# Loading W by halves and the forward tables in two ways in a fused Fourier layer and expert MLP

## The chip, the cores and the metric

The kernel runs on one core of one Trainium2 chip. The metric is the time of the core in device microseconds (us). Several executions are timed; medians are given with the lowest and highest. The engines go by short names: PE is TensorE, ACT ScalarE, DVE VectorE, POOL GpSimd, SP SyncE. Every run lists the mean clock that TensorE was granted, as a share of full speed. One profiled execution of each kernel gives the page and the trace, whose span is some 2 us shorter than the time.

## The reference

```python
X = np.fft.rfft(x, axis=1)                      # x: 8 x 3008 x 256, float32
Yr = Xr @ w_r - Xi @ w_i + b_r                  # w_r, w_i: 256 x 256
Yi = Xr @ w_i + Xi @ w_r + b_i
Yr, Yi = soft_threshold(Yr, 0.01), soft_threshold(Yi, 0.01)
y = np.fft.irfft(Yr + 1j * Yi, n=3008, axis=1)  # then 24064 tokens of 256
r = np.maximum(y @ moe_w_in, 0.0)               # 256 -> 2048
out = (s * (r * r) + b) @ moe_w_out             # 2048 -> 256
```

## The kernel before

The transform of 3008 points is done as 94 x 32 by matmuls with constant tables. A first batch goes through a start-up stage of its own (`first_batch`); while it runs, all tables and weights are loaded. "Mixing" is the product of the transformed x with w_r and w_i (together W). After about 50 us PE goes from tile to tile of the expert MLP, with the transforms of later batches in between. The parts that matter:

```python
# start: x of batch 0 in eight pieces on the POOL queue, W whole on the SP queue
emit_load_x(0)
for w in (w_r, w_i):
    st = rpool.tile([P, DC, D], F32, name="w_st", tag="rt")
    nc.sync.dma_start(out=st, in_=w.rearrange("(c p) e -> p c e", p=P))
...
def emit_load_forward():           # compact forward table of 12 pairs, placed by copies
    nc.sync.dma_start(out=F_c.rearrange("p q r k -> p q (r k)"), in_=F_d)
    nc.sync.dma_start(out=sel_t, in_=S_d)

def emit_load_inverse():
    nc.sync.dma_start(out=T_t[:, 0:H], in_=t_d[:, 0:H])
    nc.sync.dma_start(out=F_t[:, H:], in_=f_d)
    nc.sync.dma_start(out=F_2[1], in_=f_2_d)
    t_load = nc.sync.dma_start(out=T_t[:, H:], in_=t_d[:, H:])
    ...                            # identity, last table, biases
def emit_load_weights():
    for dc in range(DC):
        nc.gpsimd.dma_start(out=w_in_t[dc], in_=moe_w_in[dc * P : (dc + 1) * P, :])
    nc.gpsimd.dma_start(out=w_out_t, in_=moe_w_out.rearrange("(mc p) d -> p mc d", p=P))
...
# first_batch: after the first DFT of x come the copies that place F_c, on ACT and DVE;
# then the next x and the expert weights, let go by the second half of F_t:
gate = nc.gpsimd.tensor_copy(out=w_in_t[0][0:1, 0:1], in_=F_t[0:1, H, 0:1])
with tc.issue_after(gate.ins):
    emit_load_x(1)
    emit_load_weights()
...
def sum_w_out():                   # on POOL (GpSimd): column sums of w_out, for the bias b
    nc.gpsimd.tensor_tensor(out=acc, in0=w_out_t[:, 0:2], in1=w_out_t[:, 2:4], op=ALU.add)
    for q in range(4, MC, 2):
        nc.gpsimd.tensor_tensor(out=acc, in0=acc, in1=w_out_t[:, q : q + 2], op=ALU.add)
    nc.gpsimd.tensor_tensor(out=w_sum, in0=acc[:, 0], in1=acc[:, 1], op=ALU.add)

def make_bias():                   # the "bias matmul": PE reads the sum
    ps = other_bank()
    nc.tensor.matmul(ps[:, 0:D], ones, w_sum, start=True, stop=True)
    ...
# in each expert tile: relu on ACT, then the square on DVE, with rt as both inputs in SBUF
nc.vector.tensor_tensor(out=gt[:, :, 0:w], in0=rt[:, :, 0:w], in1=rt[:, :, 0:w], op=ALU.mult)
```

## Time and profile before

| | before |
|---|---|
| time | 848.3 us median of 6 (847.65 to 848.57) |
| span of the trace | 846.2 us |
| PE busy | 833.9 us, 99% |
| last x lands, first mixing matmul | 13.25, 14.21 us |
| first expert matmul | 47.94 us |
| w_out landed, its sum ready, bias matmul | 40.98, 50.39, 51.99 us |
| first output tile evacuated | 63.18 us |

PE is busy for nearly all of the span, so the table follows the few moments of the first 65 us that can move its start. A row of a timeline has the start in us, the length in us, engine, line, operation, output<-input, the number of merged instructions, and in brackets how long the engine was idle before and what ended that. In the waits, a row is who waited for whom: us in total, times, longest. The times of landing are taken from the trace's DMA completion counts, the 16th of a transfer's 16.

### The profile page before, as it was taken

Reading aid. Unit: us, or ns where it says so; the run is one execution under the profiler, and the core shown is the slowest. Engines: PE = TensorE matmul, PEld = TensorE weight load, DVE = VectorE, ACT = ScalarE, POOL = GpSimd, SP = SyncE. Lnnn points to the kernel's source line nnn. Section 1 sums busy time; section 2 is a strip of 40 time slices with the busy share of each in tenths; the row PEclk is TensorE's granted clock in tenths of the full one; section 3 lists DMA queues with packets and bytes.
Section 4 is the critical chain, followed back from the end, with each engine's and each line's share of the span. In section 5 each row is a group of like instructions: output and inputs, shape, how many; then the busy total and the mean of one; then the engine's idle time right before and its main releaser. Section 6 shows DMA issues by size and latency. Waiting matters only on the chain.

```text
span 846.2 us, 17115 instructions
## 1 busy us (share of the span) xinstructions
PE 833.9 (99%) x6653; PEld 599.6 (71%) x6653; DVE 691.8 (82%) x1026; ACT 642.7 (76%) x864; POOL 46.0 (5%) x71
## 2 busy tenths in 40 slices
PE   8999999999999999999999999999999999999997
PEld 6857766777677766777677776777667777766765
DVE  5989987888878987888888888798977888776674
ACT  5988886787778787788777887788877778666673
POOL 4341000000000001000000000000000000000000
PEclk9999999999999999999999999999999999999999
DMA  8945568224762367324761247613354223411111
GB/s 201 181 142 122 122 151 212 67 72 103 173 185 57 99 169 182 96 75 108 189 170 51 78 102 199 171 41 91 101 156 122 62 78 97 112 33 38 38 44 50
DMA packets 105747, 96.06 MB, mean 114 GB/s; under 512 B 9543, under 2 KB 97483, under 8 KB 104323
## 3 DMA queue, kind: packets, MB, share of 16 engines
q1 hardware_dynamic: 99218, 80.55, 32.9%
q0 software_dynamic: 6448, 14.42, 10.7%
q8 instruction: 52, 0.85, 0.4%
q14 instruction: 29, 0.23, 0.1%
HBM read 53.52 MB, written 46.66 MB: 118 GB/s over the span
## 4 chain that ended last, share of the span: by engine, by line
PE 89%; DVE 4%; DMA 3%; ACT 3%; issue 1%; POOL 0%; DVEq 0%; ACTq 0%; SPq 0%; POOLq 0%
PE psa L840 36%; PE psh L769 36%; PE psf L635 4%; PE psf L570 2%; PE psf L621 2%; PE psf L606 2%; PE psf L718 2%; PE psf L665 2%; ACT rt L776 1%; DVE gt L783 1%; DMA vd<-v 1%; PE psm L426 1%; DMA vs<-vd 1%; DMA x<-in_x_dram 1%; DMA F_c<-dft_fwd 0%
## 5 line engine op out<-in xcount | busy, mean ns | idle before, releaser
L776 ACT ACTIVATE rt<-psh 128x1024 f32<-128x1024 f32 (+2 forms) x384 | 386.8, 1009 | 119.6 <-PE psh L769 117.8
L783 DVE TENSOR_TENSOR gt<-rt 128x1024 f16<-128x1024 f32 (+2 forms) x321 | 383.9, 1199 | 98.3 <-ACT rt L776 97.6
L840 PE MATMUL psa<-w_out_t,gt 128*128 128x256 f16 (+1 forms) x3024 | 454.6, 272 | 0.1
L840 PEld LDWEIGHTS <-gt 128*128 128x128 f16 (+1 forms) x3024 | 301.0, 101 | 187.0 <-issue 1.4
L769 PE MATMUL psh<-yt,w_in 128*128 128x512 f16 (+1 forms) x1344 | 396.3, 378 | 0.2 <-ACT rt L776 0.2
L769 PEld LDWEIGHTS <-w_in 128*128 128x128 f16 x1536 | 142.9, 98 | 28.0 <-issue 2.0
L850 DVE SCALAR_TENSOR_TENSOR ost<-psa,s_bc,bias_bc 128x512 f32<-128x512 f32 (+2 forms) x97 | 71.0, 732 | 8.3 <-PE psa L840 6.7
L780 ACT ACTIVATE gt<-rt 128x1024 f16<-128x1024 f32 (+2 forms) x63 | 66.2, 1050 | 1.0
L640 DVE TENSOR_TENSOR ring<-psf,s 128x512 f16<-128x512 f32 x84 | 57.4, 684 | 3.7 <-PE psf L635 3.1
L170 ACT CAST v<-psf 128x512 f16<-128x512 f32 x78 | 45.3, 582 | 18.7 <-PE psf L665 18.7
L170 ACT CAST xf<-psf 128x512 f16<-128x512 f32 x82 | 47.9, 585 | 10.9 <-PE psf L606 10.8
L769 PE MATMUL psh<-tail,w_in 128*128 128x512 f16 (+1 forms) x192 | 52.1, 353 | 0.0
L170 ACT CAST u<-psf 96x512 f16<-96x512 f32 x75 | 43.4, 580 | 10.9 <-PE psf L570 10.7
L635 PE MATMUL psf<-W_g,xf 128*128 128x256 f16 x336 | 50.4, 272 | 0.0
L170 ACT CAST yt<-psf 128x480 f16<-128x480 f32 (+2 forms) x73 | 37.3, 523 | 14.2 <-PE psf L718 14.2
L213 POOL DMA_DIRECT2D x<-in_x_dram x36 | 18.7, 526 | 432.4 <-PE psf L570 431.2
L570 PE MATMUL psf<-x,A_t 94*96 94x512 f16 x103 | 39.3, 381 | 1.7 <-ACT yt L170 0.5
L646 DVE TENSOR_TENSOR ring<-ring,high 128x512 f16<-128x512 f16 x84 | 35.5, 423 | 2.3
L647 DVE TENSOR_TENSOR ring<-ring 128x512 f16<-128x512 f16 x84 | 35.4, 422 | 1.9
L645 DVE TENSOR_TENSOR ring<-ring,low 128x512 f16<-128x512 f16 x84 | 35.4, 421 | 1.6
L635 PEld LDWEIGHTS <-xf 128*128 128x128 f16 x336 | 32.9, 98 | 3.9
L718 PE MATMUL psf<-C_t,vs 96*128 96x96 f16 x448 | 33.0, 205 | 0.9 <-DMA vs<-vd 0.8
(97 smaller groups left out, 500.7 us busy)
## 6 DMA issues: line engine op xcount, KB each, us to landing
out_dram<-ost SPq DMA_DIRECT2D x152, 128.0 KB
ud<-u SPq DMA_DIRECT2D x28, 384.0 KB
us<-ud SPq DMA_DIRECT2D x28, 384.0 KB
vd<-v SPq DMA_DIRECT2D x42, 256.0 KB
vs<-vd SPq DMA_DIRECT2D x14, 768.0 KB
x<-in_x_dram POOLq DMA_DIRECT2D x28, 376.0 KB, 6.5
ring<-ring SPq DMA_DIRECT2D x280, 32.0 KB
out_dram<-ost SPq DMA_DIRECT2D x16, 120.0 KB
```

What stands on the lines that cost most here:

```text
L170: return None, nc.scalar.copy(out=dst, in_=src)
L570: nc.tensor.matmul(ps[0:96, :], A_t[0:N1, :], x16[(b, c)][0:N1, j * D : (j + 2) * D], start=True, stop=True,)
L635: nc.tensor.matmul(ps[:, r, :], xt[:, 2 - r, dc], W_g[:, dc, r], start=(dc == 0), stop=(dc == DC - 1),)
L640: nc.vector.tensor_tensor(out=t, in0=ps, in1=hold[i // 2][:, i % 2].unsqueeze(1).to_broadcast([P, 2, D]), op=ALU.add,)
L646: nc.vector.tensor_tensor(out=m, in0=m, in1=high, op=ALU.min)
L718: nc.tensor.matmul(ps[:, j * 96 : (j + 1) * 96], vs[(b, h)][:, k, ec * P : (ec + 1) * P], C_t, start=True, stop=True,)
L769: nc.tensor.matmul(o, w_in_t[dc][:, mc * P : (mc + 1) * P], r, start=(dc == 0), stop=(dc == DC - 1),)
L776: nc.scalar.activation(out=rt[:, :, 0:w], in_=ps[:, :, 0:w], func=AF.Relu)
L780: nc.scalar.activation(out=gt[:, :, 0:w], in_=rt[:, :, 0:w], func=AF.Square)
L783: nc.vector.tensor_tensor(out=gt[:, :, 0:w], in0=rt[:, :, 0:w], in1=rt[:, :, 0:w], op=ALU.mult)
L840: nc.tensor.matmul(ps[0:size, h, :], gts[(ti, mc // 2)][:, mc % 2, sub * size : (sub + 1) * size], w_out_t[:, mc, :], start=(mc == 0), sto ...
L850: nc.vector.scalar_tensor_tensor(out=ost[0:size, 0:k], in0=ps[0:size, 0:k], scalar=s_bc[0:size], in1=bias_bc[0:size, 0:k], op0=ALU.mult, o ...
```

## The change

It is meant to start the mixing of batch 0 sooner. W's first half of output columns comes first and the other half behind x, since the first six of twelve mixing steps use only the first. The forward tables of the first four pairs come at once and are placed while x still arrives; those of the other eight come ready-made behind x and need no placing.

```diff
-        nc.sync.dma_start(out=st, in_=w.rearrange("(c p) e -> p c e", p=P))
+        nc.sync.dma_start(
+            out=st[:, :, 0:P], in_=w.rearrange("(c p) e -> p c e", p=P)[:, :, 0:P]
+        )
         w_st.append(st)
+    F_c = uspool.tile([P, 4, 2, N2], F16, name="F_c", tag="us")
+    nc.sync.dma_start(out=F_c.rearrange("p q r k -> p q (r k)"), in_=F_d)
 ...
-    def emit_load_forward():
 ...
-    def emit_load_inverse():
+    def emit_load_tables():
+        nc.sync.dma_start(out=F_t[:, 4:H], in_=f_d[:, 0 : H - 4])
+        nc.sync.dma_start(out=F_2[0][:, 4:H], in_=f_2_d[:, 0 : H - 4])
         nc.sync.dma_start(out=T_t[:, 0:H], in_=t_d[:, 0:H])
-        nc.sync.dma_start(out=F_t[:, H:], in_=f_d)
-        nc.sync.dma_start(out=F_2[1], in_=f_2_d)
+        for st, w in zip(w_st, (w_r, w_i)):
+            nc.sync.dma_start(
+                out=st[:, :, P:], in_=w.rearrange("(c p) e -> p c e", p=P)[:, :, P:]
+            )
+        nc.sync.dma_start(out=F_t[:, H:], in_=f_d[:, H - 4 :])
+        nc.sync.dma_start(out=F_2[1], in_=f_2_d[:, H - 4 :])
         t_load = nc.sync.dma_start(out=T_t[:, H:], in_=t_d[:, H:])
 ...
-                with tc.issue_after(last_act.ins):
-                    place_w()
-        with tc.issue_after(last_dve.ins), tc.issue_after(last_act.ins):
-            place_f()
-            place_f_2()
+                with tc.issue_after(last_act.ins), tc.issue_after(last_dve.ins):
+                    place_f()
+                    place_w(0)
 ...
+            if i == 3:
+                place_w(1)
```

The tables' build on the host, the zeroing of four pairs in place of twelve, and the small memsets that hold the loads back follow suit and are cut here.

More of the change, by code (lines that the diff above doesn't have):

```diff
@@ L123 @@
     A_d = nc.inline_tensor(first.astype(np.float16), name="dft_first").ap()
-    F_d = nc.inline_tensor(fwd[:, 0:H].astype(np.float16), name="dft_fwd").ap()
+    F_d = nc.inline_tensor(fwd[:, 0:4].astype(np.float16), name="dft_fwd").ap()
     f_all = np.zeros((P, NPAIR, 2, 2, N2))
@@ L131 @@
         t_all[r, :, i % 2] = inv[r]
-    f_2 = np.stack([-f_all[:, H:, 1], f_all[:, H:, 0]], axis=2)
+    f_2 = np.stack([-f_all[:, 4:, 1], f_all[:, 4:, 0]], axis=2)
     f_d, f_2_d, t_d = (
         nc.inline_tensor(t.reshape(P, -1, P).astype(np.float16), name=name).ap()
-        for t, name in ((f_all[:, H:], "fwd_rest"), (f_2, "fwd_rest_i"), (t_all, "dft_inv"))
+        for t, name in ((f_all[:, 4:], "fwd_rest"), (f_2, "fwd_rest_i"), (t_all, "dft_inv"))
     )
@@ L244 @@
             nc.sync.dma_start(out=b_g[r : r + 1, i], in_=bv.unsqueeze(0))
-    F_c = uspool.tile([P, H, 2, N2], F16, name="F_c", tag="us")
     F_2 = [uspool.tile([P, H, P], F16, name="F_2", tag="us") for _ in range(2)]
@@ L252 @@
     sel_t = cpool.tile([P, P], F16, name="sel_t")
+    nc.sync.dma_start(out=sel_t, in_=S_d)
     eye_t = cpool.tile([P, P], F16, name="eye_t")
@@ L264 @@
     T_t = cpool.tile([P, NPAIR, P], F16, name="T_t")
-    def emit_load_forward():
-        nc.sync.dma_start(
-            out=F_c.rearrange("p q r k -> p q (r k)"), in_=F_d
-        )
-        nc.sync.dma_start(out=sel_t, in_=S_d)
-    def emit_load_inverse():
-        nc.sync.dma_start(out=T_t[:, 0:H], in_=t_d[:, 0:H])
-        nc.sync.dma_start(out=F_t[:, H:], in_=f_d)
-        nc.sync.dma_start(out=F_2[1], in_=f_2_d)
+    def emit_load_tables():
+        nc.sync.dma_start(out=F_t[:, 4:H], in_=f_d[:, 0 : H - 4])
+        nc.sync.dma_start(out=F_2[0][:, 4:H], in_=f_2_d[:, 0 : H - 4])
+        nc.sync.dma_start(out=T_t[:, 0:H], in_=t_d[:, 0:H])
+        for st, w in zip(w_st, (w_r, w_i)):
[4 more added lines that the diff above has]
+        nc.sync.dma_start(out=F_2[1], in_=f_2_d[:, H - 4 :])
         t_load = nc.sync.dma_start(out=T_t[:, H:], in_=t_d[:, H:])
@@ L298 @@
     nc.vector.memset(neg_lam, -LAM)
-    nc.vector.memset(F_t[:, 0:H], 0.0)
-    nc.gpsimd.memset(F_2[0], 0.0)
+    nc.vector.memset(F_t[:, 0:4], 0.0)
+    nc.vector.memset(F_2[0][:, 0:4], 0.0)
     def make_bounds():
@@ L316, in blocks, with place_w @@
         return t.rearrange("p q (r a k) -> p q r a k", r=2, a=2)
-    def place_w():
+    def place_w(ec):
+        e = slice(ec * P, ec * P + P)
         for i in range(2):
-            nc.scalar.copy(out=W_t[:, :, i], in_=w_st[i])
+            nc.scalar.copy(out=W_t[:, :, i, e], in_=w_st[i][:, :, e])
     def place_f():
@@ L324, in place_f @@
             r = slice(64 * a, 64 * a + 64)
-            nc.scalar.copy(out=blocks(F_t)[r, 0:H, :, a], in_=F_c[r])
-    def place_f_2():
-        for a in range(2):
-            r = slice(64 * a, 64 * a + 64)
+            nc.scalar.copy(out=blocks(F_t)[r, 0:4, :, a], in_=F_c[r])
             nc.vector.tensor_scalar_mul(
-                out=blocks(F_2[0])[r, :, 0, a], in0=F_c[r, :, 1], scalar1=-1.0
+                out=blocks(F_2[0])[r, 0:4, 0, a], in0=F_c[r, :, 1], scalar1=-1.0
             )
-            nc.vector.tensor_copy(out=blocks(F_2[0])[r, :, 1, a], in_=F_c[r, :, 0])
+            nc.vector.tensor_copy(out=blocks(F_2[0])[r, 0:4, 1, a], in_=F_c[r, :, 0])
     w_sum = cpool.tile([P, D], F16, name="w_sum")
@@ L389, in first_batch @@
                 continue
-            if c == 0:
-                with tc.issue_after(last_dve.ins):
-                    nc.vector.memset(F_c[0:1, 0, 0, 0:1], 0.0)
-                emit_load_forward()
             if c == 2:
                 with tc.issue_after(last_dve.ins):
-                    for t in (T_t[:, 0:H], F_t[:, H:], F_2[1], T_t[:, H:]):
+                    tables = (F_t[:, 4:H], F_2[0][:, 4:H], T_t[:, 0:H])
+                    tables += tuple(st[:, :, P:] for st in w_st)
+                    for t in tables + (F_t[:, H:], F_2[1], T_t[:, H:]):
                         nc.vector.memset(t[0:1, 0, 0:1], 0.0)
-                emit_load_inverse()
+                emit_load_tables()
             if c == 1:
-                with tc.issue_after(last_act.ins):
-                    place_w()
-        with tc.issue_after(last_dve.ins), tc.issue_after(last_act.ins):
-            place_f()
-            place_f_2()
+                with tc.issue_after(last_act.ins), tc.issue_after(last_dve.ins):
+                    place_f()
+                    place_w(0)
         gate = nc.gpsimd.tensor_copy(out=w_in_t[0][0:1, 0:1], in_=F_t[0:1, H, 0:1])
```

## The prediction

> **What bounds the kernel now.** I read the page first, then the chain of waits for the first 70 us in order of time, then the timeline of the first 20 us by engine, then the DMA queues in one-microsecond windows, and last the timelines of POOL and PE from 20 to 56 us. The page says where the bound is:
>
> ```profile
> PE 833.9 (99%) x6653; PEld 599.6 (71%) x6653; DVE 691.8 (82%) x1026; ACT 642.7 (76%) x864; POOL 46.0 (5%) x71
> ...
> PE   8999999999999999999999999999999999999997
> ...
> DMA  8945568224762367324761247613354223411111
> ```
>
> PE is busy in every slice of 21 us except a little in the first and the last. From the second slice on the kernel is a PE stream that the change does not touch (the matmuls, their shapes and count stay), so nearly all of 848 us is fixed. What can move is the moment at which that stream gets going. The chain of waits of the first 18 us (start us, length us, what):
>
> ```profile
> 2.88 6.32 DMA x<-in_x_dram
> 9.26 0.34 PE psm L374 x4
> 9.60 0.18 PE psf L374 x4
> 9.80 0.56 DVE ut L174
> 10.42 4.22 DMA F_c<-dft_fwd
> 14.71 0.83 ACT F_t L325
> 15.56 0.83 ACT F_t L325
> 16.41 0.59 ACT g L432
> 17.05 0.38 PE psf L456 x4
> ```
>
> The reader is to see two things. The chain starts with the load of x, and it then leaves x for the forward table F_c: issued at 10.42 behind a DVE evacuation, landed at 14.64, placed by ACT in two copies until 16.41, and only then come ACT's half of g and the first forward DFT. The x chain runs beside it and ends almost as late. This is PE in the timeline:
>
> ```profile
> 13.30 0.34 PE L374 MATMUL psm<-A_t,x 94*128 94x96 f16 x4 [0.34 <-DMA x<-in_x_dram]
> ...
> 14.21 1.92 PE L426 MATMUL psm<-W_t,ut 128*128 128x256 f16 x16
> 16.44 0.23 PE L456 MATMUL psf<-g,F_t 128*128 128x128 f16 x1 [0.31 <-ACT F_t L325]
> ```
>
> So the last x lands at about 13.3, mixing starts at 14.21, and PE stands for 0.31 us at 16.44 and again until 17.05, for the placing of F_t and the g that ACT does after it. From 17.4 to 31.5 the chain is PE almost alone, in steps of about 1.66 us (forward DFTs start at 19.92, 21.57, 23.25, 25.05), which is PE's own work: mix 8 x 0.109, forward 8 x 0.055 plus 0.11, inverse 4 x 0.055, together 1.64 us. From 31.8 to 49 it is DVE and ACT evacuations back to back, then PE. A saving before 17 us is carried along these links unless some other arrival holds one of them.
>
> [...] from 3 to 6 us the x queue and the SP queue together have 111%, 104% and 115% of 16 engines, and from 6 to 12 us x alone has 96 to 113%. So x is bound by DMA engine time and W takes from it. [...] The halves of W have runs of exactly 512 B. In this trace's packet records 512 B packets of the SP queue have a median of 27 ns and 1024 B ones 46 ns: 85% of the rate per byte, so halves are worth nearly half. [...] F_c's issue takes 0.36 us and its landing 4.2. [...]
>
> **The change, part by part.** *W in halves and an early small F_c.* Before: 512 packets of 1024 B, 512 x 46 ns / 16 engines = 1.47 us of all engines. After: 512 of 512 B and F_c's 128 of 512 B, 640 x 27 / 16 = 1.08 us. Of this a part runs before x's first packet (3.1 us), some 0.40 us before and, at the same packets per us, 0.25 after. In x's stretch that leaves 1.07 against 0.83: x gains 0.24 us. The old F_c also sent about 43 packets of 1536 B (65 ns) beside the last of x, 43 x 65 / 16 = 0.17 us; the tables that take its place are issued at about 12.0 and their first packets come 1.0 to 1.5 us later, after x. Together x ends **0.4 us** earlier, mixing starts at about 13.8.
>
> *Placing out of the way.* The two ACT copies of 0.83 us and the four DVE ones of 0.25 move from behind x to about 10 us, with a third of the columns. With half of W that is an estimated 1.4 us on ACT at 10 us, where it has a 0.48 us evacuation per 1.05 us and four banks to catch up. After mixing starts nothing but g stands ahead of the forward DFT. Before, from 14.21 to the end of the first forward DFT (last matmul issued 17.21) were 3.06 us. After: 16 mix matmuls 1.85 us, then 0.55 us, 2.40. Gain **0.66 us**. It needs the other eight pairs by the second forward DFT at about 17.1. Issued at 12.0 to 12.8, 256 packets of 2048 B, with 1.37 us per 384 KB (median landing to landing of the four tables before): estimated landed by 15.5, slowest engine 16.2. In time. T_t needs 17.3 to 17.8 against use at 17.7: just in time.
>
> *Second halves of W.* Two ACT copies of 128x256 f32 (0.48 us each, 0.36 apart, as L351 has them) go into step 3, where ACT is about 90% busy. ACT has no F_t copies behind it now and had idle of 0.44 us at 23.45; I charge **0.15 us**. W_t's first half loses the same from idle time, worth nothing.
>
> Sum: 0.4 + 0.66 - 0.15 = about **0.9 us**, 0.1% of the time.
>
> **Rivals.** *The expert weights become the wait.* The tables behind x grow by 768 KB (eight pairs twice, W's halves) ahead of F_t's second half, which gates the loads of the next x and the weights. At 1.37 us per 384 KB that is 2.7 us, less 0.4 for the earlier start and what idle DMA time absorbs: w_out lands 1.5 to 2.5 us later. POOL's sum of w_out starts on that landing and its result is read by one matmul (L349) in PE's order:
>
> ```profile
> 41.05 1.15 POOL L340 TENSOR_TENSOR acc<-w_out_t 128x512 f32<-128x512 f16 x1 [5.29 <-DMA w_out_t<-in_moe_w_out_dram]
> 42.28 7.31 POOL L344 TENSOR_TENSOR acc<-acc,w_out_t 128x512 f32<-128x512 f32 x6
> 49.67 0.72 POOL L345 TENSOR_TENSOR w_sum<-acc 128x256 f16<-128x256 f32 x1
> ```
>
> ```profile
> 51.99 0.27 PE L349 MATMUL psa<-w_sum,ones 128*128 128x256 f16 x1
> ```
>
> The sum ends at 50.39 and PE reads it at 51.99: 1.6 us of slack, which an earlier PE (0.9) and a later load (1.5 to 2.5) overdraw by 0.8 to 1.8. PE would then stand there, everything behind it is PE work, and the time is 848.0 to 849.0. Against it: the place of L349 in PE's order is not that of the source (it ran before most of the matmuls listed ahead of it), so it can fall later in the new order, and its result is not used until 63.18. I give this rival about four in ten for some loss, and half of that for losing all of the gain.
>
> *T_t or W's second half land late.* Then PE or ACT waits a few tenths at 17 to 20 us: 847.5 to 848. For it: a slowest engine trailed the median by 0.5 to 1.1 us in these loads. Against: the need is also in rough balance.
>
> *Hidden anyway.* If x does not speed up because the 640 small packets disturb it as much as 512 larger ones, only 0.5 us is left: 847.6. *Better than I count:* if x ends earlier by all of the 256 KB less and the steps up to 31 us also lose their small stalls, 1.5 us: 846.6. A new order of PE's instructions may also shift later stages by about a microsecond either way.
>
> **Range and chances.** 848.15 - 0.9 = 847.25 without a new wait. With the first rival at its weight I stay near that, at **847.3 us**. The lower end is the better case with a lucky order, 845.8; the upper the stand at L349, 848.9. A change of 2% is 17 us, as much as the whole stretch before the PE stream, so I give faster 0.01, within 2% 0.98, slower 0.01.
>
> **What would show it.** Right: the last L374 group at about 12.9 and the first L426 at 13.8 (x step); L456 at about 2 us after the first L426 with no wait for F_t, and the second forward DFT by 17.2 (placing); no ACT gap at the copies of W in step 3. F_c gone from the chain, PE in its place from about 14 us. POOL's first sum of w_out starts at 42.5 to 43.5; PE waits at L349 or not, which decides between gain and none. Wrong: x landing as late as now, a PE wait on F_t or T_t before 20 us, an ACT wait for the second half of W, or a DVE and ACT stretch between 31 and 49 us that gives the lead back.

## The result

The changed kernel took 853.58 us in the median of 6 runs (850.01 to 857.07), against 848.3 before. Executions over 1.5% slower than the fastest of the same kernel are left out of the means. Ratios here are the mean time of one kernel's runs over the mean of the other's in the same rounds, so they are not quite the ratio of the medians quoted. This one is 1.0062 (95% interval 1.0034 to 1.0091): some 5 us slower, less than 2% but clear of noise, and outside the predicted range of 845.8 to 848.9. The spread of 7 us, against 0.9 us before, is part of the result.

The page of the changed kernel (engine busy us and share; then the chain that ended last):

```profile
PE 835.0 (98%) x6653; PEld 600.0 (70%) x6653; DVE 695.0 (82%) x1030; ACT 641.7 (75%) x866; POOL 48.8 (6%) x70
...
PE 85%; DMA 5%; DVE 4%; POOL 2%; ACT 2%; issue 1%; SPq 0%; DVEq 0%; POOLq 0%; ACTq 0%
```

PE has the same 6653 matmuls and 1.1 us more busy time; the span is 5.0 us longer. POOL, with 2% of the chain, had 0% before. The chain of waits of the first 70 us names the links:

```profile
14.46 5.18 DMA F_t<-fwd_rest
...
20.29 2.06 POOL x L213 x4
22.35 1.11 POOL w_in L295 x2
23.46 20.51 DMA w_out_t<-in_moe_w_out_dram
...
50.19 2.02 POOL acc L345
52.28 2.02 POOL acc L345
54.38 1.60 POOL w_sum L346
55.98 0.04 issue
56.02 0.37 PE psa L350
```

F_c has gone from the chain. In its place stand the second half of F_t (it gates the next loads), the load of w_out, POOL's sum of it, and the bias matmul (L350, L349 before). On PE:

```profile
13.37 1.92 PE L423 MATMUL psm<-W_t,ut 128*128 128x256 f16 x16
...
49.37 1.94 PE L768 MATMUL psh<-yt,w_in 128*128 128x512 f16 x8 [0.17 <-ACT rt L775]
56.02 0.37 PE L350 MATMUL psa<-w_sum,ones 128*128 128x256 f16 x1 [4.71 <-POOL w_sum L346]
56.18 0.64 PE L839 MATMUL psa<-w_out_t,gt 128*128 128x256 f16 x2
56.61 1.91 PE L768 MATMUL psh<-yt,w_in 128*128 128x512 f16 x4
```

Mixing starts 0.84 us earlier than before, as meant. Then PE stands 4.71 us at the bias matmul, and after it four expert matmuls take 1.91 us where they took 1.02. Side by side:

| us from the start | before | changed | difference |
|---|---|---|---|
| first mixing matmul | 14.21 | 13.37 | -0.84 |
| second forward DFT | 18.14 | 16.56 | -1.58 |
| second inverse DFT | 20.70 | 19.87 | -0.83 |
| first expert matmul | 47.94 | 47.09 | -0.85 |
| gate for the next x and the weights | 17.33 | 19.77 | +2.44 |
| w_out landed | 40.98 | 43.97 | +2.99 |
| sum of w_out ready | 50.39 | 55.97 | +5.58 |
| bias matmul | 51.99 | 56.02 | +4.03 |
| first output tile evacuated | 63.18 | 68.65 | +5.47 |
| output tiles from 138 us on | | | +4.74 to +4.78 |

The second row against the third shows where half of the early lead went (-1.58 becomes -0.83): ACT stood for the second half of W, in the timeline of ACT:

```profile
18.09 0.41 ACT L325 CAST W_t<-w_st 128x256 f16<-128x256 f32 x1 [0.75 <-DMA w_st<-in_w_r_dram]
18.41 0.68 ACT L458 ACTIVATE m<-psf,neg_lam 128x512 f32<-128x512 f32 x1
18.99 0.39 ACT L325 CAST W_t<-w_st 128x256 f16<-128x256 f32 x1
```

The copies stand ahead of and behind an activation that the next inverse DFT waits for, and PE stood 0.59 us for it at 19.87. The remaining lead of 0.85 us is what was forecast; what follows undoes it. POOL's sum, in its timeline of the changed kernel:

```profile
44.04 1.15 POOL L341 TENSOR_TENSOR acc<-w_out_t 128x512 f32<-128x512 f16 x1 [9.13 <-DMA w_out_t<-in_moe_w_out_dram]
45.27 9.03 POOL L345 TENSOR_TENSOR acc<-acc,w_out_t 128x512 f32<-128x512 f32 x6
54.38 1.59 POOL L346 TENSOR_TENSOR w_sum<-acc 128x256 f16<-128x256 f32 x1
```

It starts 2.99 us later and takes 2.59 us longer than before (11.93 against 9.34), because from 49.35 us on each of its adds is slow (2.02 us for 1.16). The wait adds up: 2.99 + 2.59 + 0.85 of lead - 1.60 of slack that the sum had before = 4.83 us, against 4.71 seen.

The third cost, after the later load and the slower sum, is PE's clock. The windows show it (length, then busy us and instructions of PE, weight loads, DVE, ACT, POOL, then granted clock, DMA share, GB/s):

```profile
48.00:51.30 3.30, 3.13 (x14) 1.24 (x13) 2.12 (x3) 3.01 (x4) 3.14 (x3) 1.00 0.40 119
51.30:56.00 4.70, 0.01 (x1) 0.00 (x0) 4.70 (x3) 1.24 (x2) 4.51 (x3) 1.00 0.44 129
56.00:59.50 3.50, 3.48 (x11) 1.58 (x11) 1.05 (x1) 1.42 (x2) 0.00 (x0) 0.51 1.10 304
59.50:63.00 3.50, 3.50 (x20) 1.78 (x19) 3.05 (x3) 3.02 (x5) 1.37 (x3) 1.00 0.32 85
```

After 4.71 us without work PE gets half of its clock (0.50) for 3.41 us, worth an estimated 1.7 us of work, half of that time; the difference grows by 1.44 us there, from +4.03 to +5.47. From 63 us on the two traces keep their distance to within 0.04 us but for one place at about 131 us, where PE waits for batch 1's return from memory (vs<-vd): 0.8 us in this trace of before, none in that of the changed kernel, and between 0 and 1.9 us in the traces of all kernels here. It is noise, and it limits what a single run can tell.

### The profile page after: what moved, and what is told of

It reads as the page before. A ratio compares the mean times of both kernels' runs of the same rounds, so it can differ in the third digit from the quotient of the medians.

```text
span 851.2 us, 17130 instructions
## 1 busy us (share of the span) xinstructions
PE 835.0 (98%) x6653; PEld 600.0 (70%) x6653; DVE 695.0 (82%) x1030; ACT 641.7 (75%) x866; POOL 48.8 (6%) x70
## 4 chain that ended last, share of the span: by engine, by line
PE 85%; DMA 5%; DVE 4%; POOL 2%; ACT 2%; issue 1%; SPq 0%; DVEq 0%; POOLq 0%; ACTq 0%
PE psa L839 36%; PE psh L768 35%; PE psf L634 4%; PE psf L569 2%; DMA w_out_t<-in_moe_w_out_dram 2%; PE psf L620 2%; PE psf L605 2%; PE psf L717 2%; PE psf L664 2%; DVE gt L782 2%; ACT rt L775 1%; POOL acc L345 1%; DMA x<-in_x_dram 1%; POOL x L213 1%; DMA ring<-ring 1%
```

## The experiments

Two theories stood at the start. A: the loss is PE's wait for w_out and its sum, brought on by the 768 KB that now stand ahead of the gate. B: it comes from somewhere else in the change (the halves of W, the ACT wait, crowded loads), and the wait only marks it. All kernels but the three that add idle work for measurement are full versions; all gave correct results. Each used one chip, with its own runs of before: chip 12 for e1 to e4 (before 848.52), 9 for e5 to e8 (848.26), 8 for e9 and e10 (848.09), 15 for e11 and e12 (847.75).

**e1, the bias matmul later in PE's order.**

```diff
-    plan.setdefault(15, []).append(make_bias)
+    plan.setdefault(22, []).append(make_bias)     # and issued after the last second matmul before it
```

> The changed kernel with one matmul moved: the one that reads the sum of w_out stands about 50 PE instructions later (inside tile 0's second matmuls, still ahead of the first output). Theory A (the loss is the wait of PE for w_out's landing and POOL's sum, 4.7 us in the trace): the wait is gone, PE keeps the 0.85 us that it was ahead at its first expert matmul, 847.4 us (846.8 to 848.2), and the spread of 7 us between runs shrinks below 1.5 us. Theory B (the loss comes from elsewhere, as the wait for the second half of W or slower loads in general, and the wait only marks it): 852 to 854 us, spread as now. If POOL's sum is slowed by VectorE's squares [...], its adds stay at 2.0 us wherever they overlap those.

850.21 us (849.65 to 853.47), ratio 1.003 (1.0013 to 1.0046). The wait is gone (the matmul comes at 63.18, the sum is ready at 55.75) and the granted clock is 1.00 all through 46 to 64 us. So the time falls from 853.6 to 850.2, but not to 847.4, and the spread of 3.8 us is not under 1.5: my expectation missed by 3 us. POOL is as slow as before, without any wait of PE beside it:

```profile
45.02 9.07 POOL L345 TENSOR_TENSOR acc<-acc,w_out_t 128x512 f32<-128x512 f32 x6
54.16 1.59 POOL L346 TENSOR_TENSOR w_sum<-acc 128x256 f16<-128x256 f32 x1
```

DVE pays too: its first ten squares take 13.90 us in this trace (49.74 to 63.64) and 11.49 in that of before, PE waits 1.8 us for ACT and for squares, and the first output tile is evacuated at 65.30, 2.12 us later than before. That is about what is left of the loss. e7 measures this collision of sum and squares alone.

**e2, the kernel before with 768 KB of idle loads ahead of the gate.** Two tables are loaded into the place of w_out before w_out itself.

```diff
         nc.sync.dma_start(out=T_t[:, 0:H], in_=t_d[:, 0:H])
+        for k in range(2):
+            nc.sync.dma_start(out=w_out_t[:, 6 * k : 6 * k + 6]..., in_=t_d[:, 0:H]...)
```

> The kernel before with 768 KB of idle loads (two 384 KB tables into w_out's place) ahead of the second half of F_t, and nothing else of the change. Theory A: the gate opens 2.4 to 3 us later, w_out lands about 3 us later (44 us), POOL's sum runs into the squares and ends near 56, the bias matmul waits about 4 us: 852 to 855 us, with a spread of some us. Theory B (the loss comes from the halves of W or the placing): 848.3 to 849.

850.1 us (848.98 to 854.86), ratio 1.0026 (1.0006 to 1.0045). In its trace the gate opens at 21.52, 4.2 us later than before, w_out lands at 43.18 (+2.2), and the sum is ready at 53.46; PE waits 0.6 us. It reaches its first expert matmul at 48.71, itself 0.77 later than before, as the second forward tables came late. The sign and the spread are the forecast ones, but the size missed (852 to 855 expected): this kernel has no lead that would bring PE to the matmul sooner, so the wait is short (0.6 us) and nothing falls to half clock there (1.00 all through 46 to 64 us). Bytes ahead of the gate are enough to make the kernel slower, with no other part of the change; they don't give the whole loss. Nor do they act by the gate alone: PE itself stood 0.76 us for a table at 22.42, which it did not in the changed kernel, so e2 by itself does not separate the two ways. e3 does.

**e3, the changed kernel with w_out loaded ahead of w_in.** Two statements swap; every engine but POOL keeps its order.

```diff
+        nc.gpsimd.dma_start(out=w_out_t, in_=moe_w_out.rearrange("(mc p) d -> p mc d", p=P))
         for dc in range(DC):
             nc.gpsimd.dma_start(out=w_in_t[dc], in_=moe_w_in[dc * P : (dc + 1) * P, :])
-        nc.gpsimd.dma_start(out=w_out_t, in_=moe_w_out.rearrange("(mc p) d -> p mc d", p=P))
```

> The changed kernel with w_out loaded ahead of w_in; the order of all engines but POOL's three issues is the same. Theory A: w_out lands some 5 us or more earlier (36 to 39 us), the sum ends before 50 us at 1.2 us an add, no wait at the bias matmul, w_in lands by 44 us against use at 47: 847.4 us (846.8 to 848.2), small spread. Theory B: 852 to 854. If w_in lands after 47 us, PE waits there instead and the time rises by that wait.

848.0 us (847.28 to 848.74), ratio 0.9992 (0.998 to 1.0004). w_out lands at 39.68 and w_in at 44.65 against use at 48.08. POOL and PE, each from its timeline:

```profile
39.76 1.15 POOL L341 TENSOR_TENSOR acc<-w_out_t 128x512 f32<-128x512 f16 x1 [3.85 <-DMA w_out_t<-in_moe_w_out_dram]
40.99 7.31 POOL L345 TENSOR_TENSOR acc<-acc,w_out_t 128x512 f32<-128x512 f32 x6
48.37 0.72 POOL L346 TENSOR_TENSOR w_sum<-acc 128x256 f16<-128x256 f32 x1
...
52.13 0.27 PE L350 MATMUL psa<-w_sum,ones 128*128 128x256 f16 x1
```

The adds are at 1.2 us again, there is no wait, and the whole loss is gone, with all of the change still in. Theory A holds for the loss. The lead of PE is gone as well in this trace (first expert matmul 48.08): ACT stood 1.33 us for the second half of W, and T_t kept PE another 0.5.

**e4, the control: the same swap in the kernel before.**

> Control: the kernel before with w_out loaded ahead of w_in. Theory A: the sum was ready 1.6 us before its matmul already, so nothing changes: 848.3 us within 0.4. If the swap helps by itself (the sum off the squares frees VectorE, or the load is cheaper in this order): 847.5 or less, and then e3 proves less.

848.08 us (847.51 to 849.05), ratio 0.9995 (0.9983 to 1.0006). The sum is ready at 45.52, long before its use at 52.04, and nothing is gained: the swap is no improvement of its own, so e3 against the changed kernel measures the late sum: the wait for it, and what it does beside the squares.

**e5, the table part alone** (W whole at the start, placed by two ACT copies at 10 us).

> The changed kernel with W whole at the start, as before the change: the table part alone. Theory A: no ACT wait for W, x ends 0.2 to 0.4 us later than in the changed kernel, the gate opens about 0.9 us earlier (256 KB less ahead of it), w_out lands near 43, the sum still meets the squares and PE still waits at the bias matmul, but 1 to 2 us less: 850 to 852 us. If the halves of W were the main cause: 848 or less.

Five fast runs of 850.54 to 855.7 (one run at a granted clock of 0.557 took 1464.57 us; being the profiled one, its trace is not used), median of the fast ones 851.56, ratio 1.005 (1.0033 to 1.0067). The table part has most of the loss (the whole change had 1.0062, and 1.0044 in e10).

**e6, the W part alone**, in the kernel before.

> The kernel before with W in halves alone, second halves behind the first inverse table, placed in step 3 as in the change. Theory A: w_out lands about 0.9 us later, inside the 1.6 us of slack of the sum, so no wait at the bias matmul; x ends 0.2 us earlier and ACT does not wait or little, as the step comes 1.6 us later than in the changed kernel: 848.0 to 848.8. If the halves are the main cause: 850 or more.

848.52 us (848.26 to 850.39), ratio 1.0009 (0.9997 to 1.0021): no difference to be told. In its trace w_out lands at 41.71 (+0.7), the sum is ready at 52.00 and the bias matmul comes at 52.05. The slack of 1.6 us is just used up, and the sum's last step has already met the squares (1.59 us for 0.72).

**e7, four idle POOL adds behind the sum**, in the kernel before; nobody reads their result.

```diff
+        for q in range(4, 12, 2):
+            nc.gpsimd.tensor_tensor(out=acc, in0=acc, in1=w_out_t[:, q : q + 2], op=ALU.add)
```

> The kernel before with four more POOL adds after the sum, whose result nobody reads; the order of the other engines is the same. They run from 50.4 us beside VectorE's squares. If POOL adds and squares shut each other out: adds of 2.0 us instead of 1.16, squares of 1.9 instead of 1.15 for some 8 us, PE waits for squares or ACT, and the time rises by 1 to 2.5 us, to 849.5 to 851. If not (the long adds of the changed kernel had another cause): adds of 1.2 us, 848.3 us within 0.4.

851.9 us (851.42 to 852.56), ratio 1.0046 (1.0034 to 1.0058): +3.6 us, more than I allowed, for four instructions on an engine that is 5% busy. The squares of DVE in the kernel before, from its timeline:

```profile
50.20 11.49 DVE L783 TENSOR_TENSOR gt<-rt 128x1024 f16<-128x1024 f32 x10 [1.18 <-ACT rt L776]
```

and here, with POOL's idle adds and PE's longest wait:

```profile
50.45 15.24 DVE L785 TENSOR_TENSOR gt<-rt 128x1024 f16<-128x1024 f32 x10 [1.18 <-ACT rt L778]
...
50.35 7.45 POOL L347 TENSOR_TENSOR acc<-acc,w_out_t 128x512 f32<-128x512 f32 x4
...
PE psa L842 <- DVE gt L785: 2.9, 4, 0.8
```

Ten squares take 3.75 us longer, nearly in turn with the adds: their starts follow each other every 2.09 us (50.45, 52.52, 54.61, 56.71) as long as POOL adds, and every 1.14 after. PE then waits for squares, four times, 0.8 us at the longest, without losing its clock (1.00 all through 46 to 64 us). A pair takes 2.09 us, 0.2 less than add and square take one after the other when each runs alone (1.16 + 1.14 = 2.30). The traces show that the two hold each other up, and not by what. This is the cost that e1 kept.

**e8, the swap with W's second half behind all tables, placed in step 5.**

```diff
+            for st, w in zip(w_st, (w_r, w_i)):       # behind T_t's second half
+                nc.sync.dma_start(out=st[:, :, P:], in_=...[:, :, P:])
-            if i == 3:
+            if i == 5:
                 place_w(1)
```

> The changed kernel with w_out ahead of w_in, the second halves of W loaded behind all tables, and their ACT copies in step 5. Theory: e3 lost its lead because ACT stood 0.75 to 1.3 us for the second half of W; here it does not, the gate opens 0.9 us earlier, and PE keeps 1.2 to 1.6 us of lead at the first expert matmul (46.4 to 46.8 us against 47.9): 846.7 to 847.3 us. If tables still come too late at the faster pace (T_t or the second forward tables): 847.5 to 848.

847.39 us (846.59 to 848.73), ratio 0.9993 (0.998 to 1.0006). The first expert matmul comes at 47.11, not at 46.4 to 46.8. ACT's wait for W is down to 0.33 us, but its copies still stand around the activation:

```profile
21.33 0.41 ACT L325 CAST W_t<-w_st 128x256 f16<-128x256 f32 x1 [0.33 <-DMA w_st<-in_w_r_dram]
21.64 0.68 ACT L458 ACTIVATE m<-psf,neg_lam 128x512 f32<-128x512 f32 x1
22.23 0.39 ACT L325 CAST W_t<-w_st 128x256 f16<-128x256 f32 x1
...
23.11 0.40 PE L471 MATMUL psa<-T_t,z 128*128 128x128 f16 x4 [0.49 <-DVE z L460]
```

PE stands 0.49 us behind them. Mixing starts at 13.60 here, 0.4 to 0.6 us before the two traces with W whole below (14.19 and 14.04), but the first expert matmul comes only 0.2 us before theirs: the mixing steps take back most of what the halves gain at the start. The traced run was the slowest of the five and had the longest wait at 131 us (1.9 us).

**e9 and e12, the table part with the swap and W whole**, the version that the runs before point to.

> The table part alone (W whole at the start, both ACT copies at 10 us) with w_out loaded ahead of w_in. Theory: nothing of W stands in ACT's order in the mixing steps, so PE keeps the lead that the placing gives: the first forward DFT ends 1.1 to 1.4 us earlier than before and stays so, the first expert matmul at 46.6 to 46.9 us against 47.9; the sum ends before 50 us. 847.0 us (846.4 to 847.6). If W's halves were worth having: not below e8's 847.4. The wait for batch 1's round trip at about 131 us (0 to 1.9 us in the traces so far, in all kernels) can hide part of it in single runs.

> The kernel of e9 again, on another chip if it falls so, to see whether its lead of 0.5 us in medians (0.9 in the one trace) is there: 847.0 to 847.8 us and 0.3 to 1.0 below the runs of before. If it is chance, the ratio is 1.000 or over.

847.56 us (847.42 to 850.89), ratio 0.9995 (0.9974 to 1.0015), and on another chip 847.88 us (847.27 to 848.1), ratio 0.9999 (0.9986 to 1.0011). No engine waits for a table, the sum is ready at 46.28 and 46.01, and the first expert matmul comes at 47.33 and 47.30, 0.6 us earlier than in the trace of before. It beats the changed kernel clearly; against the kernel before no gain in time is shown. The lead itself fell short: 0.6 us at the first expert matmul, where I expected 1.0 to 1.3. The intervals reach 1.1 to 1.7 us to either side, so a gain of 0.5 to 1 us is neither shown nor ruled out. Where the 0.6 us go is open: both the wait at 131 us and the start itself (last x lands between 12.71 and 13.40 us in the six traces with W whole) vary by as much.

**e10, the changed kernel again.**

> The changed kernel unaltered, on the same chip as e9 and against the same runs of before, for its spread and its median: 850 to 857 us, median near 853. If the 7 us of spread belong to the landing of w_out, a run with an earlier landing shows a shorter wait at the bias matmul and shorter adds; if this chip gives 848, the loss is not the kernel's.

852.57 us (849.66 to 855.05), ratio 1.0044 (1.0021 to 1.0066), with a wait of 4.52 us at the bias matmul and w_out landed at 43.74. Together with the first six, twelve runs of this kernel can be sorted by their granted clock: 849.66 and 850.01 us at 1.000 and 0.999; 851.35 to 852.99 (four) at 0.998; 851.21 to 857.07 (six) at 0.994 to 0.996. The spread goes with the mean clock. In the two traced runs, both at 0.998, the lost clock is one stretch of 3.4 us at 0.50 (half of it is 1.7 of 851 us); that the runs at lower means had more of it is an estimate from this, as none of them was traced. The clock alone does not set the time, though: on this chip the kernel before also had runs at 0.996 to 0.998, of 847.92 to 852.33 us, and none of these was traced. Only two traces show the wait itself, so that the landing of w_out sets it in every run is not shown.

**e11, idle matmuls ahead of the bias matmul**, to keep PE busy in the wait.

```diff
+        for _ in range(80):
+            mm = nc.tensor.matmul(ps[:, 0:P], ones, ones, start=True, stop=True)
```

> The changed kernel with 80 idle matmuls of 128x128 (about 4.4 us of PE at full clock) ahead of the bias matmul. The build also lets 14 expert matmuls pass it, so by then PE has done 3 us of useful work more. Theory: the sum ends near 56 us as before, PE comes to the bias matmul at about 58.5 us without a wait, so no stretch at half clock follows (3.4 us at 0.50 in the changed kernel's trace, worth 1.7 us): 850.5 to 851.5 us, spread under 2 us, granted clock 0.999 or 1.000 in all runs. If the half clock does not come from PE's wait: it shows again near 56 to 62 us, 852 to 854 us, with runs at 0.994 to 0.998 as before.

853.32 us (852.69 to 855.81), ratio 1.0068 (1.0055 to 1.0082). The clock was as expected: 1.000, 0.999, 1.000, 1.000 in four runs, 0.997 in the fifth. The time was not. The sum was ready at 54.30, the 68 idle matmuls that stood together (3.96 us) began only at 56.98, after PE had waited for ACT behind slowed squares, and the bias matmul came at 60.78. So without the idle stretch (PE stood 0.65 us at the longest from 46 to 70 us) there was no half clock in the trace, as in e1, but filling it with idle work saved nothing: the time is that of the changed kernel within noise (ratios of 1.0062 and 1.0044).

The changed kernel's trace has 3.41 us at 0.50 after 4.71 us of wait, e10's has 3.4 us after 4.52 us, and e1's has none without the wait.

## Why the prediction was wrong

The step that failed is the weighing of the first rival: a later sum of w_out was to overdraw its slack of 1.6 us by 0.8 to 1.8 us, with four chances in ten, and to cost no more than that. PE stood 4.71 us at the bias matmul, because the sum was not only later but also longer, and after the wait PE lost its clock as well. Term by term:

- *x and placing.* Right. Mixing was 0.84 us earlier in this trace for 0.4 forecast, but over the traces it is less: the last x lands at 12.4 to 12.8 with halves (seven traces, median 12.64) and 12.7 to 13.4 with W whole (six, median 13.16), 0.5 us. (In the trace of before packets of 512 B took 27 ns and those of 1024 B 46 ns, 85% of the rate per byte.) Placing gave 0.74 more (-1.58 in all), for 0.66.
- *W's second half.* The step that gave it 0.15 us failed; 0.75 us of the lead was lost. It held that ACT had idle time enough; ACT stood 0.75 us for the landing (1.33 in e3), and even where it hardly waits, the copies sit around an activation that PE's next inverse DFT needs (e8). By this and the larger start the forecast lead of 0.9 us at the first expert matmul came out at 0.85, so that number was right by luck: two of its terms were off, in opposite directions.
- *The expert weights become the wait.* This rival is what happened, and it was mis-weighted and mis-sized. I gave it four in ten and 848.0 to 849.0 us. I let the bias matmul's place count against it ("it can fall later in the new order"); it kept its place, after the same sixteen expert matmuls. I had w_out 1.5 to 2.5 us later; it was 2.99 and 2.76 in the two traces, with the gate at +2.44.
- *The sum as a fixed 9.3 us.* The larger of the missing terms. A later sum runs beside the squares, and each holds the other up: 2.59 us more for the sum (e10 the same: 11.9), and 3.75 us for ten squares where nobody waits for the sum (e7). I did not ask what a later sum would run beside.
- *The wait as a plain shift.* The other missing term: PE after 4.71 us of idleness was at half clock for 3.41 us, which took the difference from +4.03 to +5.47.
- *What the parts cost together.* Without the wait but with the collision 850.2 (e1), without both 848.0 (e3), with both 852.6 to 853.6. The three mechanisms are shown each by its own trace; how the 7 us of spread divide among them is not.

## What to carry to other kernels

Before bytes are moved behind a critical load, follow everything that is gated behind them to its reader, and subtract from its slack both the delay and the lead that the reader gains. Then ask what a shifted piece of work will run beside: four adds on an engine that is 5% busy cost 3.6 us here by meeting another engine's squares (e7), and PE's waits of 4.5 to 4.7 us cost it half of its clock for 3.4 us as well (changed kernel, e10). Order loads by when their readers need them, not by how they are listed: here one swap of w_out and w_in took away the whole loss.

## What else the traces show

- With adds of 1.16 us and squares of 1.14, a pair took 2.09 us and not 2.30 (e7), so a little of the two overlapped.
- The clock records of the changed kernel's trace are 51.20 us at 1.00 and then 3.41 us at 0.50 (56.06 to 59.47). Half clock also came after a stretch that was not empty: in e2 PE was busy for 1.76 us from 5.10 to 8.50 us, and the granted clock was 0.50 from 8.50 to 11.90. In the trace of before PE was busy for 2.27 us of the same stretch, and the clock stayed at 1.00. How busy PE must be to keep its clock is not shown.
- The 16 completions of w_out's load did not come together: 13 had come by 41.66 us in the changed kernel and the last at 43.97; in the kernel before these were 40.13 and 40.98. POOL's sum waited for the last: it started 0.07 us after it in both.
